# mLSTM cell and leaky-ReLU MLP on one core: p2 first in every group, another order of the sums of x, ScalarE's transfers from unit 8 on, mixed weights behind the masks

## The chip, the cores and the metric

The kernel runs on one core of one Trainium2 chip. Its engines are TensorE (PE, with its weight loads shown apart as PEld), VectorE (DVE), ScalarE (ACT), GpSimd (POOL) and SyncE (SP), which here only issues transfers. The metric is the time of one execution on the device in microseconds (us).

## What is computed

An mLSTM cell runs over 768 tokens of 4 batches and 8 heads (head size 40); its output, 3072 tokens of 320 values, goes through a two-layer MLP:

```
for t in range(S):                       # the cell, per batch and head
    m_new = max(f[t] + m, i[t])
    C = exp(f[t] + m - m_new) * C + exp(i[t] - m_new) * outer(v[t], k[t])
    n = exp(f[t] + m - m_new) * n + exp(i[t] - m_new) * k[t]
    y[t] = sigmoid(o[t]) * (C @ q[t]) / max(abs(n . q[t]), 1)
x = y as (4 * 768, 8 * 40)
h = x @ w_in                             # 320 -> 2048
out = maximum(0.01 * h, h) @ w_out       # 2048 -> 320
```

All values are 32-bit floats.

## The kernel before

The 768 tokens are cut into six chunks of 128. A step s = 4c + b is chunk c of batch b; a group g is the MLP on chunk g of all four batches, 512 tokens. One loop at the end of the kernel interleaves the two: pass c (1 to 6) runs the *units* of group c - 1 in the order of `ffs`, and between them the cell work of chunk c. Pass 1 has 32 units (group 0, ordinary products); passes 2 to 6 have 28 each (groups 1 to 5). `manual_schedule` keeps PE, DVE, ACT and POOL in the order in which the program issues their instructions, so each of these engines is a queue: an instruction that waits holds up all behind it. ACT's queue holds its DMA issues too.

**The MLP of groups 1 to 5** is a Strassen-Winograd product with seven block products, each in two halves n = 0, 1. The first layer's, p1 to p7, are units 0 to 13 (`fast_firsts`); the second layer's, also called p1 to p7, are units 14 to 27 (`fast_units`, in the order p1, p2, p4, p6, p7, p5, p3). In the first layer several products share a chain of PSUM banks, and later products accumulate on what the earlier ones left: p1, p6, p7 and p4 on "u", p2 on "s", p5 and p3 on "v". So the result of p1(n) must have been taken out of its banks (`keep`: two copies on ACT; or `add`: two additions on DVE, and then a leaky ReLU, `relu`, on ACT) before p6(n) may be written on them. One flag, `swapped`, sets the order: in group 1 it is p2, p1, p6, p7, p4, p5, p3, with p2 kept and p1 added; in groups 2 to 5 it is p1, p6, p7, p4, p2, p5, p3, with p1 kept and p2 added. The first layer's matmuls are L946, `add` is L975, `keep` L979, `relu` L971; the second layer's matmuls are L830.

**The sums of x** (`sums_of_x`, L928, POOL) make x3 = b22 - b12, b12 - b11 in place, x2 and x4 out of the blocks of x, three instructions each, issued after the last unit of the group before. p6 reads x2, p7 x3, p4 x4.

**The sums of weights** (`sums_of_weights`, DVE, L908 to L918) are 14 instructions made once, three after each unit of pass 1 from unit 24 on; the last two are L918. **The mixed weights** (`mixed_weights`, POOL, L203 to L206: t3, a12 in place, t2, t4) are four instructions made once in pass 2, one after each of units 10 to 13; the second layer's p4 reads t4, p6 t2 and p7 t3.

**The cell work** of a pass is nine calls: u_parts of two steps after unit 1 (matmuls L629 and L634, then on DVE L639, L639 and L610 for each), u_mix of the two after unit 4 (matmuls L710, then on DVE the chain from L717 to L728, with L606 and L724 on POOL and the tanh L497 on ACT), u_parts of the other two after unit 13, the transposed gates (L332, L337) and u_mix of these after unit 17. From chunk 2 on, `prep_kq` (DVE: L516, L516, L524, L524) prepares a step's operands in pieces of one instruction, so many after each unit; `prep_exp` (L461, ACT) makes a step's exponentials three a unit, after a number of units set in `late`; `prep_mask` (L453, POOL) adds a mask to a step's w before unit 0 (second pair of the chunk) and before unit 12 (first pair of the next chunk), once w has landed. The gates of the next chunk (L283 to L303, DVE) are issued after unit 3 in pass 2 and after unit 0 in later passes.

**The second layer's DVE steps** are L848 and L853 (after p1; block sums of the activations), L857 (after p2), L879 (after p4; p7 reads its result) and L865 (after p6).

**Transfers from ACT's queue** (`feed_slowly`, in `chores`) load w, k and v for the steps four ahead: 14 for each pair of steps, queued when the pair's u_mix is done (units 4 and 17), w first; one is issued after each unit, in pass 2 only from unit 7 on.

Of the kernel before, what the change touches and what calls it, by code (L numbers as in the profile page):

```python
# [13 lines left out]
ALU = mybir.AluOpType  # L14
# [4 lines left out]
def kernel(  # L19
# [26 lines left out]
    nc = tc.nc  # L46
    B, H, S, D = q.shape
    P = 128
# [144 lines left out]
    at = 3 * KH * NH  # L193
    s4_at = raw_l[:, at : at + 8 * P].rearrange("p (n k e t) -> p n k e t", n=2, k=2, e=2)
    dw = raw_l[:, at + 8 * P : at + 12 * P].rearrange("p (n e t) -> p n e t", n=2, e=2)
    x4_at = raw_l[:, at + 12 * P : at + 12 * P + 2 * HT].rearrange("p (k t) -> p k t", t=HT)
    p1_at = [raw_l[:, at + 12 * P + 2 * HT + n * NH :][:, :NH] for n in range(2)]

    def mixed_weights():
# [720 lines left out]
    def sums_of_x(g):  # L920

        xT = st["xT", g]
        for what in range(4):
            for rows, k, a, b in alike:
                b11, b12, b21, b22 = (xT[rows, j, ts(i, HT)] for j in (a, b) for i in range(2))
                x2, x3, x4 = (t[rows, k] for t in (x2_at, x3_at, x4_at))
                to, left, right = ((x3, b22, b12), (b12, b12, b11), (x2, b22, b12), (x4, b21, x2))[what]
                nc.gpsimd.tensor_tensor(to, left, right, op=ALU.subtract)  # L928

    def fast_firsts(g):  # L930

        xT = st["xT", g]
        kept = {}

        def product(n, terms, of):
            if of not in kept:
                kept[of] = [psf.tile([P, 2, HT], F32, name=f"ph{r}", tag="mm")[:] for r in range(2)]
                first = True
            else:
                first = False  # L940
            bank = kept[of]
            for e in range(2):
                for m, (left, right) in enumerate(terms):
                    for r in range(2):
                        rows = ts(r, DP)
                        nc.tensor.matmul(  # L946
                            bank[r][:, e, :], lhsT=left(r)[rows, e], rhs=right(r)[rows],
                            start=first and e == 0 and m == 0, stop=e == 1 and m == len(terms) - 1, skip_group_check=True,
                        )
            return bank  # L950

        def w_at(i, n, at):
            return [lambda r, k=k: w5[:, 2 * i + n, at[r][k]] for k in range(2)]

        def s_at(t, n):
            return [lambda r, k=k: t[:, n, k] for k in range(2)]

        def x_at(at, h):
            return [lambda r, k=k: xT[:, at[r][k], ts(h, HT)] for k in range(2)]

        def t_of(t):
            return [lambda r, k=k: t[:, k] for k in range(2)]

        def rest(i, n, h):
            return [(lambda r: w5[:, 2 * i + n, KX[r]] if i < 2 else dw[:, n], lambda r: xT[:, KX[r], ts(h, HT)])]

        def at(n, i, h):
            return acts[:, KH * i + 4 * n : KH * i + 4 * n + 4, ts(h, HT)]

        def relu(to, z):  # L970
            nc.scalar.activation(to, z, AF.Prelu, alpha=0.01)  # L971

        def add(to, bank):
            for r in range(2):
                nc.vector.tensor_tensor(to[:, 2 * r : 2 * r + 2], to[:, 2 * r : 2 * r + 2], bank[r], op=ALU.add)  # L975

        def keep(to, bank):
            for r in range(2):
                nc.scalar.copy(to[:, 2 * r : 2 * r + 2], bank[r])  # L979

        swapped = g == 1

        def p1(n):
            z = at(n, 0, 0)
            bank = product(n, list(zip(w_at(0, n, K1), x_at(K1, 0))), ("u", n))
            if swapped:
                add(z, bank)
                relu(z, z)
            else:
                keep(z, bank)  # L990

        def p6(n):
            keep(at(n, 0, 1), product(n, list(zip(s_at(s2_at, n), t_of(x2_at))), ("u", n)))

        def p7(n):
            keep(at(n, 1, 1), product(n, list(zip(s_at(s3_at, n), t_of(x3_at))), ("u", n)))

        def p4(n):
            bank = product(n, list(zip(w_at(1, n, K2), t_of(x4_at))) + rest(1, n, 0), ("u", n))
            for r in range(2):  # L1000
                relu(at(n, 1, 0)[:, 2 * r : 2 * r + 2], bank[r])

        def p2(n):
            z = at(n, 0, 0)
            bank = product(n, list(zip(w_at(0, n, K2), x_at(K2, 0))) + rest(0, n, 0), ("s", n))
            if swapped:
                keep(z, bank)
            else:
                add(z, bank)
                relu(z, z)  # L1010

        def p5(n):
            z = at(n, 1, 1)
            add(z, product(n, list(zip(w_at(1, n, K1), x_at(K1, 1))) + rest(1, n, 1), ("v", n)))
            relu(z, z)

        def p3(n):
            z = at(n, 0, 1)
            add(z, product(n, list(zip(s_at(s4_at, n), x_at(K2, 1))) + rest(2, n, 1), ("v", n)))
            relu(z, z)  # L1020

        order = (p2, p1, p6, p7, p4, p5, p3) if swapped else (p1, p6, p7, p4, p2, p5, p3)
        return [lambda p=p, n=n: p(n) for p in order for n in range(2)]

    def u_gates(c):
        gates_T(c, bus.pop(c)[0])
# [20 lines left out]
    def ahead(s):  # L1047

        if s < NS:
            if s < 2 * B:  # L1050
                u_split(s)
            if s >= 2 * B:
                late[s] = 5 if 2 * B + 2 <= s < 3 * B else 3
            lazy[s] = prep_exp(s)
            if s < 2 * B:
                prep_qs(s)
                load_next(s)
            else:
                fine[s] = prep_kq(s)
            state_next(s, 0)  # L1060
            prep_vu(s)
            if s + 1 <= 2 * B:
                prep_mask(s + 1)
# [104 lines left out]
    with tc.manual_schedule(engines={E.PE, E.DVE, E.Activation, E.Pool}):  # L1168
# [23 lines left out]
        for c in range(1, NB + 1):  # L1192
# [6 lines left out]
            for i in range(n_ff):  # L1199
# [14 lines left out]
                    if c * B + n < NS:  # L1214
                        prep_mask(c * B + n)
                ffs[i]()
                for _ in range(1 if c > 2 and i < N1 else 2 if i > 5 else 0):
                    while fine and next(fine[min(fine)], fine) is fine:
                        del fine[min(fine)]
                if c == 1 and i >= 24:  # L1220
                    run(sums, 3)
                if c == 2 and i == 10:
                    mixes = mixed_weights()
                if c == 2 and i >= 10:
                    next(mixes, None)
                if i == n_ff - 1 and c < NB:
                    sums_of_x(c)
                if chores and (c != 2 or i > 6):
                    while chores and next(chores[0], chores) is chores:
                        chores.pop(0)  # L1230
                if c + 1 < NB:
                    if i == (1, 3, 0)[min(c, 3) - 1]:
                        gates(c + 1)
                    if i == (3, 4, 2)[min(c, 3) - 1]:
                        gates_exp(c + 1)
                upto = min(n_c, sum(p <= i for p in (place if c == 1 else pairs)))
# [65 lines left out]
```

## Time and profile before

| | before |
|---|---|
| runs | 495.93, 500.71 and 500.74 us; median 500.71 |
| profiled execution | 496.93 us, span 495.1 us, mean granted PE clock 0.972 |
| PE busy | 480.3 us (97%) |
| DVE busy | 353.7 us (71%) |
| ACT busy | 203.7 us (41%) |
| POOL busy | 199.8 us (40%) |
| group 1, first layer | 138.8 to 183.3 us of the span |
| group 2, first layer | 216.85 to 254.6 us |
| group 5, first layer | 430.1 to 461.45 us |

The span is the time from the first to the last instruction of the profiled execution; the execution's own time is 1.83 us longer. Rows of the trace give the start of a group of instructions in us from the span's start, their busy time, engine, line, operation, what is written from what, shapes and number; in square brackets stand the idle time of the engine before them and what ended it. A name such as L946 is line 946 of the kernel before.

### The profile page before, as it was taken

Reading aid. Unit: us, or ns where it says so; the run is one execution under the profiler, and the core shown is the slowest. Engines: PE = TensorE matmul, PEld = TensorE weight load, DVE = VectorE, ACT = ScalarE, POOL = GpSimd, SP = SyncE. Lnnn points to the kernel's source line nnn. Section 1 sums busy time; section 2 is a strip of 40 time slices with the busy share of each in tenths; the row PEclk is TensorE's granted clock in tenths of the full one; section 3 lists DMA queues with packets and bytes.
Section 4 is the critical chain, followed back from the end, with each engine's and each line's share of the span. In section 5 each row is a group of like instructions: output and inputs, shape, how many; then the busy total and the mean of one; then the engine's idle time right before and its main releaser. Section 6 shows DMA issues by size and latency. Waiting matters only on the chain.

```text
span 495.1 us, 14022 instructions
## 1 busy us (share of the span) xinstructions
PE 480.3 (97%) x5621; PEld 433.5 (88%) x5621; DVE 353.7 (71%) x585; ACT 203.7 (41%) x508; POOL 199.8 (40%) x239
## 2 busy tenths in 40 slices
PE   8997999999998899999999999999999999999997
PEld 7896788867787789998899998899989899988997
DVE  4759998898999967786787886787737787104641
ACT  3465865742635351155631335620344611153210
POOL 4142743452385961494412694203583003700020
PEclk9568999999999989999999999999999999999999
DMA  9977786898761573486584685663865211200001
GB/s 115 161 193 160 168 209 163 173 187 169 158 142 26 135 149 80 115 167 151 145 152 96 150 170 118 174 124 93 156 161 128 54 56 46 87 1 1 2 1 54
DMA packets 165297, 59.31 MB, mean 120 GB/s; under 512 B 128816, under 2 KB 156016, under 8 KB 165232
## 3 DMA queue, kind: packets, MB, share of 16 engines
q1 hardware_dynamic: 125104, 51.20, 46.0%
q10 hardware_dynamic: 40128, 7.21, 9.2%
q8 instruction: 44, 0.72, 0.6%
q14 instruction: 21, 0.17, 0.1%
HBM read 51.68 MB, written 6.70 MB: 118 GB/s over the span
## 4 chain that ended last, share of the span: by engine, by line
PE 70%; DVE 11%; SPq 9%; DMA 4%; ACT 3%; issue 2%; POOL 0%; ACTq 0%; DVEq 0%; POOLq 0%
PE po L830 31%; PE ph L946 27%; SPq L233 4%; PE pT L710 3%; PE sd L629 2%; PE po L796 2%; SPq L358 2%; PE ph L774 2%; DVE qn L524 1%; SPq L372 1%; DVE qn L639 1%; ACT kqT L554 1%; PE sd L634 1%; DMA w<-a_dr 1%; DMA rb<-in_q_dram 1%
## 5 line engine op out<-in xcount | busy, mean ns | idle before, releaser
L830 PE MATMUL po<-w_out,acts 128*128 128x160 f32 x640 | 89.1, 300 | 0.0
L830 PEld LDWEIGHTS po<-w_out,acts 128*128 128x128 f32 x640 | 87.3, 190 | 0.6 <-ACT acts L971 0.3
L946 PE MATMUL ph<-xT,w_in 64*128 64x256 f32 x720 | 82.7, 378 | 0.0
L946 PEld LDWEIGHTS ph<-xT,w_in 64*128 64x128 f32 x720 | 69.2, 187 | 8.9 <-issue 0.7
L975 DVE TENSOR_TENSOR acts<-acts,ph 128x512 f32<-128x512 f32 x60 | 38.3, 682 | 41.6 <-PE ph L946 41.5
L830 PE MATMUL po<-raw,acts 128*128 128x160 f32 x480 | 66.4, 300 | 0.0
L830 PEld LDWEIGHTS po<-raw,acts 128*128 128x128 f32 x480 | 65.4, 190 | 0.3
L606 POOL TENSOR_TENSOR S<-S,f 40x336 f32<-40x336 f32 x36 | 31.6, 879 | 75.7 <-PE pT L710 35.9
L461 ACT ACTIVATE w<-w,gT 128x64 f32<-128x64 f32 (+1 forms) x192 | 51.7, 346 | 15.7 <-DMA w<-a_dr 4.6
L979 ACT COPY acts<-ph 128x512 f32<-128x512 f32 x60 | 32.1, 587 | 46.7 <-PE ph L946 46.7
L971 ACT ACTIVATE acts<-acts 128x1024 f32<-128x1024 f32 x30 | 31.7, 1056 | 43.6 <-DVE acts L975 43.4
L774 PE MATMUL ph<-xT,w_in 64*128 64x256 f32 x320 | 38.6, 392 | 1.2 <-ACT acts L782 1.2
L946 PE MATMUL ph<-acts,w 64*128 64x256 f32 x320 | 37.5, 382 | 1.8 <-DVE acts L975 1.8
L453 POOL TENSOR_TENSOR w<-w,i 128x512 f32<-128x512 f32 x20 | 27.7, 1394 | 26.2 <-DMA w<-a_dr 14.3
L774 PEld LDWEIGHTS ph<-xT,w_in 64*128 64x128 f32 x320 | 31.6, 193 | 5.7 <-ACT acts L782 1.6
L796 PE MATMUL po<-w_out,acts 128*128 128x320 f32 x128 | 36.5, 437 | 0.0
L946 PEld LDWEIGHTS ph<-acts,w 64*128 64x128 f32 x320 | 31.2, 187 | 5.7 <-POOL w L453 2.2
L724 POOL TENSOR_TENSOR xb<-xb,den 128x320 f32<-128x320 f32 x16 | 11.6, 727 | 60.5 <-DVE xb L721 58.1
L639 DVE TENSOR_TENSOR qn<-w,sd 64x512 f32<-64x512 f32 x40 | 27.3, 684 | 8.2 <-PE sd L629 4.5
L796 PEld LDWEIGHTS po<-w_out,acts 128*128 128x128 f32 x128 | 23.6, 190 | 9.3 <-issue 0.3
L863 POOL TENSOR_TENSOR y<-y,raw 128x160 f32<-128x160 f32 x10 | 9.5, 950 | 54.5 <-DVE acts L865 44.0
L946 PE MATMUL ph<-xT,raw 64*128 64x256 f32 x240 | 29.0, 394 | 1.7 <-DVE acts L975 1.7
(169 smaller groups left out, 810.8 us busy)
## 6 DMA issues: line engine op xcount, KB each, us to landing
rb<-in_k_dram SPq DMA_DIRECT2D x64, 80.0 KB
rb<-in_q_dram SPq DMA_DIRECT2D x64, 80.0 KB
rb<-in_o_gate_dram SPq DMA_DIRECT2D x64, 80.0 KB
ea<-a_dr SPq DMA_DIRECT2D x32, 128.0 KB
raw<-in_moe_w_out_dram SPq DMA_DIRECT2D x6, 640.0 KB
w<-a_dr ACTq DMA_DIRECT2D x24, 128.0 KB
xT<-x_dr SPq DMA_DIRECT2D x32, 96.0 KB
acts<-in_moe_w_in_dram SPq DMA_DIRECT2D x20, 128.0 KB
```

The lines of the kernel that those rows point to most:

```text
L233: nc.sync.dma_start(to[DP * r : DP * (r + 1), 2 * P * slot : 2 * P * (slot + 1)], src[r, :, SLOTS[r][slot], :],)
L453: nc.gpsimd.tensor_tensor(w, w, cm2.unsqueeze(1).to_broadcast([P, H, SL]), op=ALU.add)
L461: yield nc.scalar.activation(w[:, h, :], w[:, h, :], AF.Exp, bias=gT[c][:, 0, bh : bh + 1], scale=1.0)
L606: nc.gpsimd.tensor_tensor(new, old, g, op=ALU.mult)
L639: nc.vector.tensor_tensor(mixed(s)[toks, u], w[toks], bank[1 - u][toks], op=ALU.mult)
L774: nc.tensor.matmul(ph[r][:, cols], lhsT=w_row(r, slot, j), rhs=xT[DP * r : DP * (r + 1), slot, cols], start=(slot == 0), stop=(slot == KC ...
L796: nc.tensor.matmul(po[n][:], lhsT=acts[:, f, ts(n, P)], rhs=w_out[:, f, :], start=(f == 0), stop=(f == NF - 1),)
L830: nc.tensor.matmul(bank[:], lhsT=left[:, f, :], rhs=right[:, f, :], start=f == 0, stop=f == KH - 1)
L946: nc.tensor.matmul(bank[r][:, e, :], lhsT=left(r)[rows, e], rhs=right(r)[rows], start=first and e == 0 and m == 0, stop=e == 1 and m == le ...
L971: nc.scalar.activation(to, z, AF.Prelu, alpha=0.01)
L975: nc.vector.tensor_tensor(to[:, 2 * r : 2 * r + 2], to[:, 2 * r : 2 * r + 2], bank[r], op=ALU.add)
L979: nc.scalar.copy(to[:, 2 * r : 2 * r + 2], bank[r])
```

## The change

`swapped` is gone: every group from 1 on has the order p2, p1, p6, p7, p4, p5, p3, keeps p2 (ACT) and adds p1 (DVE). The sums of x become x1 = b12 - b11 (in the place where x4 was), x2 = b22 - x1 and x3 = b22 - b12, nine instructions at the end of the group before; the fourth, b21 - x2, is made in place by `last_sum_of_x` right after p2(1), which reads b21 unchanged. p4 now reads b21's place, p5 reads x1.

In the loop, the pieces of `prep_kq` come one a unit before unit 14 and two after, in every pass (before: in pass 2 none to unit 5, then two). Of the weight sums of pass 1 the last two (L918) are issued in pass 2 after unit 3, behind the gates. The four mixed weights are issued together after unit 12 of pass 2, behind both masks of that unit. ACT's transfers are issued from unit 8 on: one a unit to unit 13, then two. In `late`, steps 14, 15, 18, 19, 22 and 23 get 5 units in place of 3.

The instructions of each engine stay the same in kind and number, apart from the order and the operands named here; the order of SP's queue does not change.

```diff
--- before.py
+++ after.py
@@ -193,7 +193,7 @@
     at = 3 * KH * NH
     s4_at = raw_l[:, at : at + 8 * P].rearrange("p (n k e t) -> p n k e t", n=2, k=2, e=2)
     dw = raw_l[:, at + 8 * P : at + 12 * P].rearrange("p (n e t) -> p n e t", n=2, e=2)
-    x4_at = raw_l[:, at + 12 * P : at + 12 * P + 2 * HT].rearrange("p (k t) -> p k t", t=HT)
+    x1_at = raw_l[:, at + 12 * P : at + 12 * P + 2 * HT].rearrange("p (k t) -> p k t", t=HT)
     p1_at = [raw_l[:, at + 12 * P + 2 * HT + n * NH :][:, :NH] for n in range(2)]
 
     def mixed_weights():
@@ -920,12 +920,18 @@
     def sums_of_x(g):
 
         xT = st["xT", g]
-        for what in range(4):
+        for what in range(3):
             for rows, k, a, b in alike:
-                b11, b12, b21, b22 = (xT[rows, j, ts(i, HT)] for j in (a, b) for i in range(2))
-                x2, x3, x4 = (t[rows, k] for t in (x2_at, x3_at, x4_at))
-                to, left, right = ((x3, b22, b12), (b12, b12, b11), (x2, b22, b12), (x4, b21, x2))[what]
+                b11, b12, b22 = xT[rows, a, :HT], xT[rows, a, HT:], xT[rows, b, HT:]
+                x1, x2, x3 = (t[rows, k] for t in (x1_at, x2_at, x3_at))
+                to, left, right = ((x1, b12, b11), (x2, b22, x1), (x3, b22, b12))[what]
                 nc.gpsimd.tensor_tensor(to, left, right, op=ALU.subtract)
+
+    def last_sum_of_x(g):
+
+        for rows, k, a, b in alike:
+            b21 = st["xT", g][rows, b, :HT]
+            nc.gpsimd.tensor_tensor(b21, b21, x2_at[rows, k], op=ALU.subtract)
 
     def fast_firsts(g):
 
@@ -978,16 +984,10 @@
             for r in range(2):
                 nc.scalar.copy(to[:, 2 * r : 2 * r + 2], bank[r])
 
-        swapped = g == 1
-
         def p1(n):
             z = at(n, 0, 0)
-            bank = product(n, list(zip(w_at(0, n, K1), x_at(K1, 0))), ("u", n))
-            if swapped:
-                add(z, bank)
-                relu(z, z)
-            else:
-                keep(z, bank)
+            add(z, product(n, list(zip(w_at(0, n, K1), x_at(K1, 0))), ("u", n)))
+            relu(z, z)
 
         def p6(n):
             keep(at(n, 0, 1), product(n, list(zip(s_at(s2_at, n), t_of(x2_at))), ("u", n)))
@@ -996,22 +996,18 @@
             keep(at(n, 1, 1), product(n, list(zip(s_at(s3_at, n), t_of(x3_at))), ("u", n)))
 
         def p4(n):
-            bank = product(n, list(zip(w_at(1, n, K2), t_of(x4_at))) + rest(1, n, 0), ("u", n))
+            bank = product(n, list(zip(w_at(1, n, K2), x_at(K2, 0))) + rest(1, n, 0), ("u", n))
             for r in range(2):
                 relu(at(n, 1, 0)[:, 2 * r : 2 * r + 2], bank[r])
 
         def p2(n):
-            z = at(n, 0, 0)
-            bank = product(n, list(zip(w_at(0, n, K2), x_at(K2, 0))) + rest(0, n, 0), ("s", n))
-            if swapped:
-                keep(z, bank)
-            else:
-                add(z, bank)
-                relu(z, z)
+            keep(at(n, 0, 0), product(n, list(zip(w_at(0, n, K2), x_at(K2, 0))) + rest(0, n, 0), ("s", n)))
+            if n == 1:
+                last_sum_of_x(g)
 
         def p5(n):
             z = at(n, 1, 1)
-            add(z, product(n, list(zip(w_at(1, n, K1), x_at(K1, 1))) + rest(1, n, 1), ("v", n)))
+            add(z, product(n, list(zip(w_at(1, n, K1), t_of(x1_at))) + rest(1, n, 1), ("v", n)))
             relu(z, z)
 
         def p3(n):
@@ -1019,8 +1015,7 @@
             add(z, product(n, list(zip(s_at(s4_at, n), x_at(K2, 1))) + rest(2, n, 1), ("v", n)))
             relu(z, z)
 
-        order = (p2, p1, p6, p7, p4, p5, p3) if swapped else (p1, p6, p7, p4, p2, p5, p3)
-        return [lambda p=p, n=n: p(n) for p in order for n in range(2)]
+        return [lambda p=p, n=n: p(n) for p in (p2, p1, p6, p7, p4, p5, p3) for n in range(2)]
 
     def u_gates(c):
         gates_T(c, bus.pop(c)[0])
@@ -1050,7 +1045,7 @@
             if s < 2 * B:
                 u_split(s)
             if s >= 2 * B:
-                late[s] = 5 if 2 * B + 2 <= s < 3 * B else 3
+                late[s] = 5 if s % B > 1 else 3
             lazy[s] = prep_exp(s)
             if s < 2 * B:
                 prep_qs(s)
@@ -1214,23 +1209,23 @@
                     if c * B + n < NS:
                         prep_mask(c * B + n)
                 ffs[i]()
-                for _ in range(1 if c > 2 and i < N1 else 2 if i > 5 else 0):
+                for _ in range(1 if i < N1 else 2):
                     while fine and next(fine[min(fine)], fine) is fine:
                         del fine[min(fine)]
-                if c == 1 and i >= 24:
+                if c == 1 and 24 <= i < 28:
                     run(sums, 3)
-                if c == 2 and i == 10:
-                    mixes = mixed_weights()
-                if c == 2 and i >= 10:
-                    next(mixes, None)
+                if c == 2 and i == 12:
+                    run(mixed_weights())
                 if i == n_ff - 1 and c < NB:
                     sums_of_x(c)
-                if chores and (c != 2 or i > 6):
+                for _ in range(0 if i < 8 else 1 if i < N1 else 2):
                     while chores and next(chores[0], chores) is chores:
                         chores.pop(0)
                 if c + 1 < NB:
                     if i == (1, 3, 0)[min(c, 3) - 1]:
                         gates(c + 1)
+                        if c == 2:
+                            run(sums)
                     if i == (3, 4, 2)[min(c, 3) - 1]:
                         gates_exp(c + 1)
                 upto = min(n_c, sum(p <= i for p in (place if c == 1 else pairs)))
```

## The prediction

> **What bounds the kernel now.** I read the page's first lines, then busy time by stretches, then the waits of TensorE (PE), then the rows of VectorE (DVE) and GpSimd (POOL) around those waits. The page says who is nearly always busy:
>
> ```profile
> span 495.1 us, 14022 instructions
> PE 480.3 (97%) x5621; PEld 433.5 (88%) x5621; DVE 353.7 (71%) x585; ACT 203.7 (41%) x508; POOL 199.8 (40%) x239
> ```
>
> So only PE's idle or slowed time can be won. Busy time by stretches (length, then busy time of PE, PEld, DVE, ACT, POOL, then the granted clock) shows where that is; the rows are the first-layer part of groups 1, 2, 3, 4 and 5:
>
> ```profile
> 138.80:183.30 44.50, 40.99 (x609) 35.01 (x609) 38.06 (x56) 20.90 (x47) 32.86 (x27) 0.96 0.50 117
> ...
> 216.85:254.60 37.75, 37.75 (x609) 33.50 (x608) 27.93 (x49) 20.50 (x48) 17.45 (x21) 1.00 0.68 149
> ...
> 288.15:325.90 37.75, 37.75 (x610) 33.50 (x609) 27.92 (x49) 19.85 (x44) 17.45 (x21) 1.00 0.67 155
> 359.40:397.30 37.90, 37.90 (x546) 34.08 (x545) 22.96 (x41) 19.05 (x40) 15.20 (x20) 1.00 0.48 113
> 430.10:461.45 31.35, 31.35 (x290) 27.87 (x289) 6.75 (x11) 13.90 (x21) 2.96 (x5) 1.00 0.02 7
> ```
>
> Groups 2 to 5 are solid PE at full clock. Group 1, the one that already starts with p2, is 44.50 - 37.75 = 6.75 us longer for the same products. PE's rows there:
>
> ```profile
> 151.75 2.50 PE L946 MATMUL ph<-acts,w 64*128 64x256 f32 x16 [1.81 <-DVE acts L975]
> ...
> 173.72 7.64 PE L946 MATMUL ph<-xT,raw 64*128 64x256 f32 x48 [1.71 <-DVE acts L975]
> ```
>
> The first is p6(0), waiting for the adds of p1(0) on DVE; the second is p3, waiting for the adds of p5(0), and it then runs slowly (7.64 us; 48 such matmuls take 5.2 elsewhere: 31.35/290 each). Why DVE is late, DVE first, then POOL:
>
> ```profile
> 147.29 1.38 DVE L639 TENSOR_TENSOR qn<-w,sd 64x512 f32<-64x512 f32 x2
> ...
> 150.94 2.47 DVE L975 TENSOR_TENSOR acts<-acts,ph 128x512 f32<-128x512 f32 x4
> ...
> 167.69 5.26 DVE L524 TENSOR_TENSOR qn<-kqT,ea 64x512 f32<-64x512 f32 x2
> 172.97 2.48 DVE L975 TENSOR_TENSOR acts<-acts,ph 128x512 f32<-128x512 f32 x4
> ```
>
> ```profile
> 165.73 3.35 POOL L203 TENSOR_TENSOR raw<-w_out 128x1280 f32<-128x1280 f32 x1
> 169.16 3.23 POOL L204 TENSOR_TENSOR w_out<-w_out 128x1280 f32<-128x1280 f32 x1
> 172.35 1.72 POOL L453 TENSOR_TENSOR w<-w,i 128x512 f32<-128x512 f32 x1
> 178.16 1.27 POOL L453 TENSOR_TENSOR w<-w,i 128x512 f32<-128x512 f32 x1 [4.09 <-DMA rb<-in_k_dram]
> 179.39 2.92 POOL L205 TENSOR_TENSOR raw<-w_out 128x1280 f32<-128x1280 f32 x1
> 182.38 2.92 POOL L206 TENSOR_TENSOR raw<-w_out,raw 128x1280 f32<-128x1280 f32 x1
> ```
>
> Two L524, 0.72 each by their median, took 5.26 us while POOL mixed weights (L203, L204), and the pair ends 0.56 after L204 does: each waited out a whole POOL instruction. The last two mixes, L205 and L206, met only DVE work that reads PSUM (L975, L639), and nothing was slowed.
>
> **Part 1: group 1's late adds.** Two L918 (2.25 us) leave DVE's queue before group 1 and return behind gates(3). L639 then starts when its matmuls allow: 1.35 after u_parts' start at 144.17 (group 2: 221.82 - 220.47), at 145.5 and not 147.29. Lower down, L203 and L204 no longer lie beside L524, and DVE's cell steps go one a unit, so p5's adds come in time as in groups 2 to 4. If all of that goes: -6.75. Bounds: -4.0 (p3's wait and slow matmuls alone: 1.88 + 2.1) and -6.75.
>
> **Part 2: p2, p1, p6 in groups 2 to 5.** PE's matmuls are the same. Before, p1's banks were emptied by ScalarE copies (0.59 each), with u_parts between p1 and p6. After, u_parts sits between p2 and p1, and p6(0) waits for DVE's adds of p1(0), queued behind L639 x2, L610, L639 x2, L610. With u_parts starting at U: L639 at U+1.35, queue empty at U+5.05 (group 2: 225.5 - 220.47), adds until U+6.3. PE is ready for p6 at U + 2.1 (u_parts) + 3.5 (p1) = U+5.6. In group 1, p6(0) ended 1.9 after its second add (152.2 to 154.1), so now at U+8.2 against U+7.35 undisturbed: 0.9 late. The same holds in group 1. Groups 1 to 4: +3.6. Group 5 has no u_parts: the adds (1.3) fit under p1(1) (1.7), but ScalarE now has two relus of 1.06 ahead of p6(0)'s copy, and p7(0) needs that: +0.3. Bounds a group: 0 (adds in time) and 2.6 (what group 1 paid: p6(0) at 154.1, not 151.5).
>
> **Part 3: sums of x.** Nine POOL subtractions at the group's end, not twelve, then three after p2(1). x2, the first that PE needs, is sixth, not ninth, and p6 comes later: hidden, cost 0. The three late ones (0.85 each) wait for p2(1); queued behind them is u_mix's state step, which waits for PE until some 5 us later. p7(1) and p4 need them over 10 us later. If that cover went, p4 would wait by what is missing.
>
> **Part 4: ScalarE's transfers.** None before unit 8, one to unit 13, then two. The same 28 issues a group at 0.4 to 0.7 us. They leave units 0 to 7, where ScalarE empties PE's banks; before, no copy there made PE wait in groups 2 to 5, so nothing is won. Six value transfers now stand in a row ahead of the tanh (L497): three took 2.25 us (at 259.27), six take 4.5, the tanh ends near 264.7, and L721 wants it at 266.8. Cost 0; bounds 0 and a rival below. `late` moves the exponentials of steps 14, 15, 18, 19, 22 and 23 two units on, still ahead of u_parts: 0. SyncE's queue keeps its order, instruction for instruction.
>
> **Part 5: the mixes behind the masks.** The second mask of unit 12 needs the fourth w transfer, issued at relu p5(1). Call the PE end of p5(1) E. In this program that is about 170.0: 144.2 + u_parts 2.1 + p1 3.5 + p6(0) 2.6 + u_mix 2.1 + 72 slots of 0.216 (p6(1), p7, p4, p5). Then adds to E+1.9, transfer 3.8 (174.30 to the mask at 178.16), mask 1.27: the mixes start near E+7.1. Alone they last 11.7 (4 x 2.92). DVE reaches L848 at U' + 5.1 = E+10.3 (U' is u_parts at E+5.2). L848 x2 and L853 x2 read SBUF twice, like L524, so I take them to alternate with the mixes: two L848 (1.13) slip between, the mixes end at E+7.1+11.7+2.3, less 0.4 for hand-overs (L524, once free, took 0.56 and not 0.72): E+20.7. PE wants t4 for p4(0) at E + 5.2 (p3) + 2.1 + 8.95 (p1, p2) + 2.65 = E+18.9: wait **1.8**. The two L853, L606 of POOL between them and the four small DVE steps end near E+24.4; before, that point was free at 193.3, with PE's p4(0) at 194.9. From u_mix's first transpose (L717, 194.07) to the end of the first L879 (201.75 + 1.21) are 8.9 us of DVE work: L879 ends at E+33.3. p7(0) needs it and stands 8.8 after p4(0), at E+29.5: wait **3.8**. Bounds of the two together: 0 (mixes done early) and 7.5 (the w transfer held 2.1 us, as ScalarE was between 165.35 and 167.98).
>
> What an idle PE does to its clock, by stretches of 3.4 us before and after the gaps:
>
> ```profile
> 150.30:153.70 3.40, 1.95 (x15) 1.59 (x16) 3.37 (x8) 1.32 (x2) 2.41 (x2) 1.00 0.00 0
> 170.80:174.20 3.40, 1.69 (x14) 1.03 (x10) 3.37 (x4) 0.00 (x0) 3.27 (x2) 1.00 0.71 157
> 174.20:177.60 3.40, 3.40 (x17) 2.68 (x18) 1.25 (x3) 3.31 (x8) 0.00 (x0) 0.50 0.64 174
> ```
>
> A stretch with PE busy for 1.69 was followed by half clock, one with 1.95 was not. A wait of 3.8 leaves at most 1.5 in one of the two stretches it falls in, so I add half a stretch at half clock, 3.4 / 2 = 1.7, rounded to **1.8** for hand-over. The 0.9 of part 2 trips nothing. Bounds: 0, and 3.5 (both waits trip).
>
> The Trainium skill, "TensorE: Matmul & The Clock Gate", section "What's actually happening", gives the cold state to at least one idle window of about 3.4 us. The trace differs: 1.7 us idle sufficed. By the page the sum below would be 1.8 lower, 499.7. On part 5 the skill's "SBUF — State Buffer", section "Who interferes with whom", says that a two-SBUF-input DVE instruction and a SBUF-reading GpSimd one exclude each other for the whole instruction. The trace agrees (L524: 5.26 for two); taken as a mere slowdown of 5.26/1.44 = 3.7 for the time of the mixes, the four would still end with the mixes, so the sum stays.
>
> **The sum**, against the profiled execution's own 496.93 (span 495.1 and 1.83 around it): 496.93 - 6.75 + 3.6 + 0.3 + 1.8 + 3.8 + 1.8 = **501.5**. The runs shown are 495.93, 500.71 and 500.74; the profiled one lies 3.8 below their median, and the trace can't say which step makes that difference, so I add nothing for it. Measured against the median, 500.71, the forecast is no change; 1% (about what a measurement of this kernel can tell from none) reaches from 495.7 to 505.7.
>
> **Rivals.**
> - *The mixes cost nothing* (fourth transfer early, or DVE not excluded): 496.93 - 6.75 + 3.9 = 494.1. For it: L205 and L206 cost nothing before. Against it: they ended at 185.3, a microsecond before L848; now they start where they ended. 17%.
> - *p1's adds come in time*: 501.5 - 3.6 = 497.9, if ScalarE and DVE clear their queues 0.9 earlier. Against it: L639 and L610 run back to back. 8%.
> - *Slower: p6(0) waits 2.6 in groups 2 to 4*, as in group 1 before, and half of these waits trip the clock: 501.5 + 3 x 1.7 + 2 x 1.8 = 510.2. It takes 1.7 us more DVE work ahead of L639; the gate steps (3.9 us beside POOL's sums, done at 221.1) have 2.4 to spare. 10%.
> - *Slower: the six value transfers hold the tanh*. L497 may end 0.7 after L721's time, L879's slack in group 2; that is 1.2 us a transfer. With three held 2.1 each, 2.9 a group, in four groups: 513. One was held so before, at 165.35. 8%.
> - *The change doesn't do what it says*: p3's wait stays in group 1, 501.5 + 4.0 = 505.5. 5%.
>
> **Numbers.** The sum itself gets 52%: 10 above 505.7 (both waits trip the clock, transfer held), 42 within 1%. Faster by over 1%: 17. Within: 42 + 8 + 5 = 55. Slower: 10 + 10 + 8 = 28. The range 493.5 to 507 leaves out the two slow rivals (18). The likeliest case's own range is 498 to 507.
>
> **What would show it.** Group 1's first-layer stretch near 38.6 us, without p3's wait; a wait of PE for L981 (the adds' new line) of under a microsecond at p6(0) in groups 1 to 4; L203 to L206 in a row after both masks, with L848 and L853 stretched beside them; PE idle at p4(0) and, longer, at p7(0) of group 1, half clock behind. If L848 starts before the mixes or after they end, part 5 is wrong; if p6(0) never waits, part 2 is.

## The result and the profile after

| | runs | median us | from - to |
|---|---|---|---|
| before | 6 | 499.05 | 495.93 - 503.92 |
| after | 6 | 505.01 | 504.07 - 508.41 |

The kernel after takes 1.0142 of the time before (95% interval 1.0093 to 1.0192): 1.4% slower. Every ratio here and below leaves out runs more than 1.5% above the fastest of their kernel (here before's 503.92) and is taken against runs of before made beside them, so it is not the quotient of two medians of these tables. The profiled execution of after took 508.41 us (span 506.6), the longest of its six runs; it lies 11.5 above the profiled execution of before, where the medians are 6.0 apart. In the page's first lines PE has the same work in a longer span:

```profile
span 506.6 us, 14039 instructions
...
PE 480.8 (95%) x5621; PEld 434.6 (86%) x5621; DVE 362.1 (71%) x585; ACT 202.5 (40%) x508; POOL 201.2 (40%) x239
```

Busy time by stretches of after (length, then PE, PEld, DVE, ACT, POOL, granted clock, DMA share and GB/s): group 1's first and second layer, then the first layers of groups 2 to 5.

```profile
143.19:182.12 38.93, 38.92 (x609) 34.71 (x608) 33.08 (x55) 19.68 (x46) 20.75 (x23) 1.00 0.41 105
182.12:225.88 43.76, 36.03 (x298) 35.42 (x294) 36.89 (x44) 8.17 (x28) 30.13 (x24) 0.88 0.66 124
225.88:264.41 38.53, 38.50 (x609) 33.67 (x608) 27.87 (x49) 19.76 (x44) 17.01 (x20) 1.00 0.54 129
297.93:336.46 38.53, 38.49 (x609) 33.66 (x608) 28.77 (x48) 19.64 (x44) 17.42 (x21) 1.00 0.56 137
369.98:408.44 38.46, 38.46 (x545) 33.66 (x544) 23.29 (x40) 18.91 (x40) 13.96 (x18) 1.00 0.43 103
441.28:472.86 31.58, 31.58 (x289) 30.00 (x288) 6.94 (x12) 13.79 (x21) 2.26 (x4) 1.00 0.02 7
```

The second line's counterpart before:

```profile
183.30:216.82 33.52, 33.52 (x299) 33.07 (x295) 27.40 (x44) 6.58 (x25) 16.51 (x19) 1.00 0.53 117
```

Group 1's first layer is 5.6 us shorter, the first layers of groups 2 to 5 are together 2.4 longer, and group 1's *second* layer, in which the diff moves nothing on PE, is 10.2 longer, with less than full clock. PE's rows there show one wait:

```profile
191.70 1.15 PE L710 MATMUL pT<-qn,S 128*64 128x64 f32 x32
200.58 1.98 PE L710 MATMUL pT<-qn,S 128*64 128x64 f32 x32 [7.73 <-DVE f L344]
```

The second step's transposes need the PSUM bank that held tg, and DVE's copies of tg (L342, L344) free it. They are late because of what stands ahead of them in DVE's queue. DVE, then POOL:

```profile
184.72 0.50 DVE L610 TENSOR_TENSOR S<-S,sd 40x336 f32<-40x336 f32 x1
185.14 6.92 DVE L848 TENSOR_TENSOR acts<-acts 128x1024 f32<-128x1024 f32 x2
191.98 7.72 DVE L853 TENSOR_TENSOR acts<-acts 128x1024 f32<-128x1024 f32 x2
199.63 0.54 DVE L857 TENSOR_TENSOR y<-raw,po 128x160 f32<-128x160 f32 x2
200.09 0.21 DVE L342 COPY gT<-tg 128x64 f32<-128x64 f32 x1
200.23 0.21 DVE L344 COPY f<-tg 128x64 f32<-128x64 f32 x1
```

```profile
178.24 1.27 POOL L453 TENSOR_TENSOR w<-w,i 128x512 f32<-128x512 f32 x1 [8.28 <-DMA w<-a_dr]
183.01 1.27 POOL L453 TENSOR_TENSOR w<-w,i 128x512 f32<-128x512 f32 x1 [3.50 <-DMA w<-a_dr]
184.24 2.89 POOL L203 TENSOR_TENSOR raw<-w_out 128x1280 f32<-128x1280 f32 x1
187.21 3.76 POOL L204 TENSOR_TENSOR w_out<-w_out 128x1280 f32<-128x1280 f32 x1
191.06 3.75 POOL L205 TENSOR_TENSOR raw<-w_out 128x1280 f32<-128x1280 f32 x1
194.89 3.74 POOL L206 TENSOR_TENSOR raw<-w_out,raw 128x1280 f32<-128x1280 f32 x1
```

The pairs L848 and L853 took 2.34 and 2.35 us before; now 6.92 and 7.72. The mixes begin at 184.24, 0.9 ahead of the first L848, and each mix and each addition (one L848 or L853) waits for the other's end in turn: L203 ends at 187.13, the first L848 can only then run its 1.1, L204's 3.76 hold that 0.8, and so on for four rounds. The granted clock by stretches of 3.4 us:

```profile
191.90:195.30 3.40, 0.95 (x32) 0.81 (x28) 3.40 (x2) 0.83 (x2) 3.32 (x2) 1.00 0.89 152
195.30:198.70 3.40, 0.00 (x0) 0.00 (x0) 3.40 (x2) 0.00 (x0) 3.33 (x1) 0.50 0.11 31
198.70:202.10 3.40, 1.52 (x29) 1.55 (x30) 3.30 (x10) 0.00 (x0) 1.63 (x1) 0.50 0.00 0
202.10:205.50 3.40, 3.40 (x20) 3.28 (x18) 2.87 (x7) 0.00 (x0) 1.49 (x2) 0.50 0.24 64
```

So the 10.2 us are about 7.9 of wait (7.73 and the hand-over) and 2.3 of half clock once PE works again.

Group 1 itself starts 4.4 us later in this pair of profiles (143.19 for 138.78). PE waits in pass 1 for L267 on DVE (the row is below); the next section asks whether the change makes that.

```profile
133.11 1.83 PE L796 MATMUL po<-w_out,acts 128*128 128x320 f32 x4 [3.02 <-DVE w_out L267]
```

### The profile page after: what moved, and what is told of

It reads as the page before. It is cut to its first block, busy times and chain, and to the rows that moved or that the text cites. A ratio compares the mean times of both kernels' runs of the same rounds, so it can differ in the third digit from the quotient of the medians.

```text
span 506.6 us, 14039 instructions
## 1 busy us (share of the span) xinstructions
PE 480.8 (95%) x5621; PEld 434.6 (86%) x5621; DVE 362.1 (71%) x585; ACT 202.5 (40%) x508; POOL 201.2 (40%) x239
## 4 chain that ended last, share of the span: by engine, by line
PE 76%; DVE 8%; SPq 7%; DMA 3%; issue 3%; ACT 1%; POOL 1%; ACTq 0%; DVEq 0%; POOLq 0%
PE ph L952 32%; PE po L830 29%; PE po L796 4%; PE pT L710 3%; PE sd L629 3%; PE ph L774 2%; SPq L233 2%; SPq L358 2%; DMA rb<-in_q_dram 1%; SPq L363 1%; SPq L372 1%; PE sd L634 1%; DVE raw L265 1%; DMA rb<-in_o_gate_dram 1%; DVE acts L853 1%
## 5 line engine op out<-in xcount | busy, mean ns | idle before, releaser
L830 PE MATMUL po<-w_out,acts 128*128 128x160 f32 x640 | 89.1, 300 | 0.0
L830 PEld LDWEIGHTS po<-w_out,acts 128*128 128x128 f32 x640 | 87.3, 190 | 0.6 <-issue 0.3
L952 PE MATMUL ph<-xT,w_in 64*128 64x256 f32 x720 | 86.6, 379 | 0.0
L952 PEld LDWEIGHTS ph<-xT,w_in 64*128 64x128 f32 x720 | 71.4, 187 | 8.2 <-issue 0.5
L830 PE MATMUL po<-raw,acts 128*128 128x160 f32 x480 | 67.9, 304 | 0.0
L830 PEld LDWEIGHTS po<-raw,acts 128*128 128x128 f32 x480 | 66.8, 193 | 0.3
L981 DVE TENSOR_TENSOR acts<-acts,ph 128x512 f32<-128x512 f32 x60 | 38.1, 680 | 40.2 <-PE ph L952 39.9
L453 POOL TENSOR_TENSOR w<-w,i 128x512 f32<-128x512 f32 x20 | 26.6, 1341 | 43.7 <-DMA w<-a_dr 43.3
L796 PE MATMUL po<-w_out,acts 128*128 128x320 f32 x128 | 38.1, 450 | 3.0 <-DVE w_out L267 3.0
L952 PE MATMUL ph<-acts,w 64*128 64x256 f32 x320 | 39.2, 382 | 0.1
L774 PE MATMUL ph<-xT,w_in 64*128 64x256 f32 x320 | 38.1, 390 | 0.2 <-DVE w_in L267 0.2
L639 DVE TENSOR_TENSOR qn<-w,sd 64x512 f32<-64x512 f32 x40 | 27.4, 684 | 14.8 <-PE sd L634 7.6
L952 PEld LDWEIGHTS ph<-acts,w 64*128 64x128 f32 x320 | 32.0, 187 | 5.6 <-issue 1.2
L774 PEld LDWEIGHTS ph<-xT,w_in 64*128 64x128 f32 x320 | 31.4, 192 | 4.5 <-DVE w_in L267 0.3
L524 DVE TENSOR_TENSOR qn<-kqT,ea 64x512 f32<-64x512 f32 x32 | 26.9, 841 | 0.8
```

The lines of the kernel that those rows point to most:

```text
L453: nc.gpsimd.tensor_tensor(w, w, cm2.unsqueeze(1).to_broadcast([P, H, SL]), op=ALU.add)
L524: nc.vector.tensor_tensor(mixed(s)[rows, 1 - r], d["kqT"][rows, 1].rearrange("p (h t) -> p h t", t=SL), d["ea"][rows], op=ALU.mult,)
L639: nc.vector.tensor_tensor(mixed(s)[toks, u], w[toks], bank[1 - u][toks], op=ALU.mult)
L774: nc.tensor.matmul(ph[r][:, cols], lhsT=w_row(r, slot, j), rhs=xT[DP * r : DP * (r + 1), slot, cols], start=(slot == 0), stop=(slot == KC ...
L796: nc.tensor.matmul(po[n][:], lhsT=acts[:, f, ts(n, P)], rhs=w_out[:, f, :], start=(f == 0), stop=(f == NF - 1),)
L830: nc.tensor.matmul(bank[:], lhsT=left[:, f, :], rhs=right[:, f, :], start=f == 0, stop=f == KH - 1)
```

## Experiments

Theory 1: the loss is made in group 1's second layer by the mixes beside L848 and L853, as read above. Rival 1: it is the late transfers of w from ScalarE's queue, behind which masks and mixes stand. Rival 2: it is the new order of the products, through waits at p6(0). The table has every profile's stages: start of group 1, its two layers, the first layers of groups 2 to 5 together, all in us (the other second layers are 33.52, 33.52, 32.84 and 30.69 in all of them, to 0.02). "Lead" is from the first mix to the first L848, "wait" PE's wait for L344.

| kernel | start | first | second | 2 to 5 | lead | wait | median, ratio to before (95%) |
|---|---|---|---|---|---|---|---|
| before | 138.78 | 44.52 | 33.52 | 144.69 | - | 0 | |
| before, again | 140.94 | 47.96 | 33.52 | 144.96 | - | 0 | |
| after | 143.19 | 38.93 | 43.76 | 147.10 | 0.90 | 7.73 | 505.01, 1.0142 (1.0093 - 1.0192) |
| after, again | 140.07 | 39.88 | 43.31 | 147.16 | 0.88 | 7.75 | |
| mixes ahead of masks | 144.54 | 39.56 | 33.52 | 147.10 | 16.33 | 0 | 497.23, 0.9952 (0.9914 - 0.9990) |
| mixes in halves | 141.19 | 40.08 | 39.37 | 147.09 | 1.31 | 1.77 | 502.92, 1.0075 (1.0040 - 1.0109) |
| mixes one a unit | 139.20 | 39.66 | 34.93 | 147.09 | 15.96 | 1.19 | 496.58, 0.9982 (0.9945 - 1.0018) |
| old order of products | 142.53 | 40.09 | 42.72 | 144.45 | 1.37 | 7.17 | 502.09, 1.0058 (1.0020 - 1.0095) |
| mixes alone moved, in before | 141.01 | 42.86 | 39.83 | 144.75 | 6.70 | 3.11 | 499.24, 0.9995 (0.9947 - 1.0042) |
| the same, again | 140.20 | 44.37 | 35.35 | 144.93 | 5.84 | 0 | |
| old transfers | 141.16 | 41.42 | 35.35 | 147.09 | 5.97 | 0 | 501.22, 1.0040 (1.0000 - 1.0080) |
| the same, again | 138.31 | 41.15 | 40.44 | 147.09 | 5.44 | 4.11 | |
| mixes ahead, old order | 141.78 | 40.91 | 33.52 | 144.46 | 16.34 | 0 | 495.34, 0.9924 (0.9886 - 0.9962) |
| the same, p1 first in group 1 | 139.69 | 42.50 | 33.52 | 144.48 | 19.21 | 0 | 496.87, 0.9953 (0.9920 - 0.9987) |

**Mixes ahead of the masks.**

```diff
+                if c == 2 and i == 12:
+                    run(mixed_weights())
                 for n in masks.get(i, ()) if 1 < c < NB else ():
...
-                if c == 2 and i == 12:
-                    run(mixed_weights())
```

> The kernel after, with one edit: the four mixed weights are issued at unit 12 ahead of its two masks instead of behind them. Theory 1 (the mixes run beside DVE's two-SBUF-input adds L848 and L853, each waiting for whole GpSimd instructions; L342 and L344 then free the transposes' bank late, PE waits 7.7 us for it in group 1's second layer and runs 10 us at half clock): GpSimd starts the mixes some 10 us earlier and is through before L848; group 1's second layer falls from 43.8 to 33.5-35 us; at most 1-2 us come back as a wait for p5's adds behind L524. Total 8 to 10 us below the kernel after, so 495-497, ratio to before 0.99 to 1.0. Rival 1 (the late transfers of w from ScalarE's queue are the cause, the mixes only stand behind them): the masks and what follows are as late as before, the second layer stays above 40 us, total 503-505. Rival 2 (the new order of the products is the loss, through waits at p6): total within 2 us of the kernel after, 503-506.

POOL and DVE of this run:

```profile
171.08 3.36 POOL L203 TENSOR_TENSOR raw<-w_out 128x1280 f32<-128x1280 f32 x1
174.51 2.91 POOL L204 TENSOR_TENSOR w_out<-w_out 128x1280 f32<-128x1280 f32 x1
177.50 3.23 POOL L205 TENSOR_TENSOR raw<-w_out 128x1280 f32<-128x1280 f32 x1
180.81 3.25 POOL L206 TENSOR_TENSOR raw<-w_out,raw 128x1280 f32<-128x1280 f32 x1
184.02 2.50 POOL L453 TENSOR_TENSOR w<-w,i 128x512 f32<-128x512 f32 x2
```

```profile
174.69 3.28 DVE L524 TENSOR_TENSOR qn<-kqT,ea 64x512 f32<-64x512 f32 x1
179.19 2.09 DVE L524 TENSOR_TENSOR qn<-kqT,ea 64x512 f32<-64x512 f32 x1
187.41 2.35 DVE L848 TENSOR_TENSOR acts<-acts 128x1024 f32<-128x1024 f32 x2
189.68 2.35 DVE L853 TENSOR_TENSOR acts<-acts 128x1024 f32<-128x1024 f32 x2
```

The mixes are through 3.3 us before L848; the four additions take their own time, and the second layer is 33.52, though the masks now begin only at 184.02 (178.24 in after). Two single L524, one a unit, are stretched to 3.28 and 2.09, and no addition of p5 is late for PE. Rival 1 in its plain form (late masks cost PE time) and rival 2 (only 2 us to be had) fall: one call moved ahead takes the ratio from 1.0142 to 0.9952.

**Mixes in halves.** Each mix is two instructions of 128x640, behind the masks as in after.

> The kernel after, with each of the four mixes cut into two instructions of half the columns, in the same place behind the masks. Theory 1 with the exclusion for whole instructions: each L848 and L853 waits out half a mix only, some 1.5 to 1.9 us, in place of 3.1 to 3.9; the chain of four ends 4 to 7 us earlier, PE's wait for the transposes' bank falls from 7.7 to between 1 and 4 us, the half clock behind it is shorter or gone; group 1's second layer 34.5 to 39 us, total 498-501. If DVE is only slowed in proportion to GpSimd's busy time (no exclusion by instruction), the split changes nothing: 43-44 us and 504-506. Rival 1 (late transfers): unchanged too.

```profile
193.75 1.98 PE L709 MATMUL pT<-qn,S 128*64 128x64 f32 x32 [1.77 <-DVE f L343]
197.32 3.01 PE L829 MATMUL po<-raw,acts 128*128 128x160 f32 x10 [1.59 <-POOL raw L205]
```

(Lines are numbered one lower in this kernel: L343 is L344, L709 is L710, L829 is L830; all mixes are L205.) The same work in smaller instructions cuts the wait from 7.73 to 1.77: the exclusion is by the instruction. But POOL's mixes now end 57.6 us after the group's start (55.4 in after), and p4, which PE reaches earlier, waits 1.59 for t4 (the wait that the prediction had placed there); with the two waits the granted clock falls to 0.50 (193.8 to 197.2), and the layer is 39.37, just above the range expected; the total missed it by 2 us.

**Mixes one a unit, as before.** `next(mixes)` after each of units 10 to 13.

> The kernel after, with the mixes issued one after each of units 10 to 13 as in the kernel before. Theory 1: the first two run beside L524 (two SBUF inputs as well; p5's adds late, PE's wait of 1 to 2 us at p3 returns), the last two stand behind the masks and now meet the first L848s: second layer of group 1 between 36 and 41 us, first layer 39 to 42 us; total 499-503, between the kernel after and the one with the mixes ahead of the masks. Rival 1 (late transfers alone): second layer above 42 us, total 503-506. Rival: the place of the mixes is all and the old one was free of cost: second layer 33.5, total 495-496.

Better than expected, and by its interval not to be told from before: the first two run beside L524, and still p3 does not wait. The rows suggest why, the operands' pieces come one a unit and the L524 stand apart, but no run changes that alone. Of the last two mixes, the end of one and the whole of the next meet the two L848 (the third mix begins 2.0 before them), and PE waits 1.19 for L344, with no loss of clock.

**The old order of the products** (`swapped` and the sums of x as in before, all else as in after).

> The kernel after, with the order of the products and the sums of x as in the kernel before (groups 2 to 5 begin with p1, which ScalarE copies; group 1 with p2); mixes behind the masks, transfers, the late L918 and the pace of the pieces stay as in the kernel after. Theory 1: the first layers of groups 2, 3 and 4 go back from 38.5 to 37.75 us and that of group 5 from 31.6 to 31.3; the second layer of group 1 stays near 43.8; total 2 to 3 us below the kernel after, 502-503.5. Rival 2 (the order is the main loss): total 496-499.

As theory 1 has it: groups 2 to 5 give back 2.65 us (147.10 to 144.45), the second layer of group 1 stays at 42.72 with its 7.17 of wait. The order costs about what was forecast (3.0), a quarter of what group 1's second layer loses.

**The mixes alone, in the kernel before:** together at unit 12, behind the masks.

> The kernel before, with one edit: its four mixed weights are issued together at unit 12 behind the two masks instead of one after each of units 10 to 13. Theory 1: L524 is free of the mixes, so p3's wait for p5's adds and its slow matmuls go from group 1's first layer (44.5 to 40-41.5 us); but the mixes now run from about 179 to 191 and beyond, across L848 and L853, so PE waits 4 to 8 us for the transposes' bank and the second layer goes from 33.5 to 40-44 us. Sum: 2 to 6 us above the kernel before, 501-505. Rival 1 (late transfers are the cause; here they are not gated until unit 7 and come early): mixes done in time, second layer 33.5, total 4 us below the kernel before.

Half right. p3's wait is gone and the second layer is 39.83 here, but p6(0) still waits 2.7 (42.86), and the total, expected 2 to 6 us higher, is that of before, with runs from 495.1 to 506.8. The profiled execution, 503.89, is one of the longest, so its stages need not be those of the median.

**The old transfers, in the kernel after** (`if chores and (c != 2 or i > 6):` in place of the loop from unit 8).

> The kernel after, with ScalarE's transfers paced as in the kernel before (one a unit; in pass 2 only from unit 7 on); all else as in the kernel after. Theory 1: the masks may come up to 3 us earlier and the mixes with them, but they still lie across L848 and L853; group 1's second layer falls by no more than 3-4 us, 40-44 us, total 502-505. Rival 1 (the gated transfers are the cause): mixes done before L848, second layer 33.5-35, total 495-497.

Theory 1 missed here: 35.35, not 40 to 44. The second mask starts 37.2 us after the group (39.8 in after), the mixes 6.0 before L848 and not 0.9. POOL, then DVE:

```profile
182.62 2.91 POOL L204 TENSOR_TENSOR w_out<-w_out 128x1280 f32<-128x1280 f32 x1
185.62 7.36 POOL L205 TENSOR_TENSOR raw<-w_out 128x1280 f32<-128x1280 f32 x1
193.05 2.90 POOL L206 TENSOR_TENSOR raw<-w_out,raw 128x1280 f32<-128x1280 f32 x1
```

```profile
185.60 2.35 DVE L848 TENSOR_TENSOR acts<-acts 128x1024 f32<-128x1024 f32 x2
187.87 2.35 DVE L853 TENSOR_TENSOR acts<-acts 128x1024 f32<-128x1024 f32 x2
```

Here L848 began 0.02 us ahead of L205, and DVE kept POOL out over all four additions (L205 took 7.36). PE only waited 1.76 for t4 from L206. The kernel's runs spread from 496.7 to 505.3, so this kernel and the previous one were each profiled again:

> The kernel after with ScalarE's transfers as before, unchanged, profiled once more, since its runs spread from 496.7 to 505.3 us. In the first profile the first L848 began 0.02 us ahead of the third mix, and DVE then ran all four adds in a row (1.2 us each) while that mix took 7.4 us: PE paid 1.8 us. Theory (who begins first keeps the other out): if a mix is under way again when L848 is issued, the adds and the mixes alternate, 3 to 4 us an add, and the second layer of group 1 takes 38 to 43 us; if an add is first, 35 to 36 us. Rival (with the mixes 4 us earlier the collision is always cheap): 35 to 36 us whatever the order, and the spread is that of the start of group 1.

> The kernel before with the mixes alone behind the masks, unchanged, profiled once more, since its runs spread from 495.1 to 506.8 us. First profile: mixes from 180.2, L848 issued at 186.9 while the third ran, adds and mixes alternated for two adds, second layer of group 1 39.8 us. Theory: the second layer is set by the number of mixes still to come when L848 is issued: four 43 to 44, two 39 to 40, none 33.5 us; if an add begins between two mixes, 35 to 36. Rival: 39.8 us again, whatever the places.

The old transfers again, where L848 (182.47) met L204 under way since 180.04: POOL, DVE, PE.

```profile
180.04 2.91 POOL L204 TENSOR_TENSOR w_out<-w_out 128x1280 f32<-128x1280 f32 x1
183.03 3.76 POOL L205 TENSOR_TENSOR raw<-w_out 128x1280 f32<-128x1280 f32 x1
186.87 3.76 POOL L206 TENSOR_TENSOR raw<-w_out,raw 128x1280 f32<-128x1280 f32 x1
```

```profile
182.47 5.40 DVE L848 TENSOR_TENSOR acts<-acts 128x1024 f32<-128x1024 f32 x2
187.80 5.62 DVE L853 TENSOR_TENSOR acts<-acts 128x1024 f32<-128x1024 f32 x2
```

```profile
194.30 1.98 PE L710 MATMUL pT<-qn,S 128*64 128x64 f32 x32 [4.11 <-DVE f L344]
```

The same kernel, 40.44 in place of 35.35. And the mixes alone, again, went the other way: L848 at 187.58, L205 at 187.73 and 7.24 long, second layer 35.35. So with a lead near 6 us, a few tenths decide between a wait of 1.8 and one of 3 or 4; with the lead of 0.9 that after has in both its profiles, all four additions alternate with mixes. Rival 1 thus holds a part: the gated transfers cost nothing by themselves (group 1's first layer is even shorter with them, see part 4 below), but they set the lead.

**Before and after, once more.**

> The kernel before, unchanged, profiled once more. If the spread of its runs (494.8 to 505.4 us) is made in pass 1, where the weights' transfers land, group 1 starts anywhere between 138.5 and 145 us of the span, and the stretches behind it repeat: 44.5, 33.5, 37.8, 33.5, 37.7, 33.5, 37.9, 32.8, 31.3, 30.7 us, each to 0.3. If the spread is made in group 1 itself, its first layer differs by over 1 us.

> The kernel after, unchanged, profiled once more. Theory 1: first layer of group 1 39 to 40 us, second 42 to 44 us with a wait of 6 to 8 us for the transposes' bank behind four stretched L848 and L853; groups 2 to 4 at 38.5. The start of group 1 lies anywhere between 138.5 and 145 us if the difference of 4.4 us found there between the two kernels is chance, near 143 if the change makes it.

Both places vary. The start of group 1 lies between 138.31 and 144.54 over the 14 profiles, 138.78 to 140.94 for the one kernel before, 140.07 to 143.19 for the one kernel after: two profiles of each cannot tell the 4.4 us of the first pair from chance. The wait for L267 in pass 1, 3.02 in after's first profile, stands in before's second profile too, with 2.2, so the change is not needed for it. And before's group 1 was 3.4 us longer in its second profile, with the same two waits, 5.3 us together and not 3.5, and half clock behind (the row gives total, number and longest):

```profile
PE ph L946 <- DVE acts L975: 5.3, 2, 3.5
```

**The two gains together** (mixes ahead of the masks, old order), and the same with p1 first in group 1 too:

> The kernel after, with two edits together: mixes ahead of the masks, and the order of products and sums of x of the kernel before. Theory 1, by the stages of the two runs that made one edit each: group 1 first layer 39.5-40, second 33.5; groups 2 to 4 37.7, group 5 31.3; 2.4 us below the kernel with the mixes ahead of the masks alone: 494-495.5, ratio to before 0.987-0.992. If the two gains overlap, 497.

> The same two edits, with p1 first in group 1 as well (p1 copied by ScalarE, p2 added by DVE, in all groups). Theory 1: p6(0) then waits for no adds of DVE in any group, and group 1's first layer comes to 37.8-38.5 us, 1 to 2 us below the run with p2 first in group 1: 492.5-494.5. Rival: the weights' last sums or w_in's blocks are not ready for p1 so early or ScalarE's copies stand behind other work at the start of group 1, and PE waits there instead: 496 or more.

The first is the best kernel found, 0.9924 (0.9886 to 0.9962) of before: 495.34, within what was expected, though its first layer, 40.91, is 0.9 longer than the 40 expected at most. The second took the time of its rival, but not for the rival's reasons (weight sums, w_in's blocks, ScalarE's copies): p6(0) comes so early that it waits for POOL's sums of x (L928), and half clock follows (first layer 42.50).

```profile
PE ph L946 <- POOL acts L928: 1.3, 1, 1.3
```

## Why the prediction was right or wrong

The forecast was 501.5, 4.6 us above the profiled time of before; measured was 505.01, 6.0 above the median. That lies within the stated range, 493.5 to 507, but two steps of the sum failed (parts 4 and 5), so the total is right in part by luck. By stages, with the means of the two profiles of each kernel: -6.8 (group 1's first layer), +10.0 (its second), +2.3 (groups 2 to 5) make +5.5; forecast were -5.85, +7.4 and +3.0. The 2.6 that the second layer cost beyond its forecast were partly paid back by the two others. The mean of -6.8 stands for a -5.6 in the first pair of profiles and a -8.1 in the second.

- **Part 1, -6.75: right.** The stretch was to be 38.6 with the 0.9 at the group's own p6(0); it is 38.93 and 39.88, without p3's wait. The size depends on which execution of before is taken: 44.52 or 47.96. For p3 it suffices to move the mixes (the kernel before with the mixes alone moved has no wait there). The pieces one a unit seem to suffice too (after with the mixes one a unit has no wait either), but that run differs from before in more than the pieces. The bound of 4.0 for p3 alone is 4.1 by the row shown: 1.71 of wait, not 1.88, and 7.64 less 5.2.
- **Part 2, +3.6 and +0.3: right.** +0.74, +0.80 and +0.57 in groups 2 to 4 and +0.30 in group 5, gone when the old order is put back. PE's rows of groups 2 to 5 list no wait, for its matmuls overlap; the delay shows in p6(0) itself (L981 and L952 are L975 and L946 of before; DVE, then PE, group 2):

```profile
236.22 2.47 DVE L981 TENSOR_TENSOR acts<-acts,ph 128x512 f32<-128x512 f32 x4
```

```profile
237.04 2.50 PE L952 MATMUL ph<-acts,w 64*128 64x256 f32 x16
```

The two additions of p1(0) end at 236.90 and 237.49, and p6(0) starts on the first of its banks at 237.04 and on the second at 237.55; its 16 matmuls take 2.50, where 32 take 3.73. In group 1 the wait was below 1 in the first profile and 1.3 in the second, where the weight sums that stay in pass 1 (L911) ran until 148.0, right up to L639, so that there L639 did not start "when its matmuls allow".
- **Part 3, 0: right.** No run with the new order shows a wait of PE's matmuls for the sums of x; in three of them one weight load waits 0.3 us for the last sum.
- **Part 4, 0: wrong.** The step that failed is the zero itself: the prediction has "nothing is won", and nothing lost, when the transfers leave units 0 to 7. ScalarE's queue issued the first w 27.2 us after the group's start (23.4 before), and the second mask came 2.3 to 3.5 us later than with the old transfers (39.8 and 40.8 against 37.2 and 37.5 after the group's start). Alone that costs nothing, as the run with the mixes ahead of the masks shows; with the mixes behind the masks it took their lead over L848 from some 5.7 to 0.9 us. The prediction's mixes started at E+7.1; they started at E+9.8 (E, the end of p5(1), is near 174.4). Most of that is the fourth w transfer, forecast at E+1.9 and issued at 179.45, E+5.05: ScalarE had stood on the issue of the second w from 172.09 to 174.41, and the exponentials then ran ahead of p5(1)'s relu. Something was won, too: in both profiles with the old transfers PE waits in p5 for a relu on ScalarE, 0.85 and 0.89, and group 1's first layer takes 41.42 and 41.15; in the five profiles with the same order and gated transfers that wait is not there and it takes 38.93 to 40.08.
- **Part 5, +7.4: mechanism right, place wrong.** Mixes and additions alternated as forecast. The step that failed is the list of who waits: "PE wants t4 for p4(0)" and then L879 for p7(0). DVE's queue holds something that PE wants earlier than either, the copies L342 and L344, since the second step's transposes reuse tg's bank. Ahead of them stand all four additions, so the whole delay fell on one wait of 7.73; p4 and p7 then found everything ready. The prediction followed data and forgot a bank: it did count the copies (among "the four small DVE steps" that end near E+24.4) but did not ask who waits for them. By its own figures PE would have wanted the bank a good 1 us before p4(0), near E+17.9, so its waits would have come to about 6.5 there (an estimate) instead of 1.8 and 3.8.
- **Clock, 1.8: right in size**; what the second layer lost beyond the wait is 2.3. The run with the 1.19 wait shows no half clock. The prediction's reading, that the busy time of a stretch tells, does not hold up (last section).
- **Rivals.** In the second layers of groups 2 to 5, 33.52, 33.52, 32.84 and 30.69 before and after, no wait for the tanh appears, so the six value transfers held nothing up. (The price of that rival does not follow from its terms: three times 2.1, less 2.8 of slack, is 3.5 a group, not 2.9.) Nor did p6(0) wait 2.6 anywhere in after.
- **The level.** The sum was taken against an execution 3.8 below the median of the runs shown and read as "no change" against that median. What makes before's two profiles differ is mostly the length of group 1's first layer (3.4 us), which the change cuts, and the start of group 1 (2.2), which it leaves. With +5.5 on the median of before, 499.05, the stages give 504.5, half a microsecond from the measured 505.01; with two profiles of each kernel, part of that closeness is chance. Of the 3.5 us between forecast and result, 2.1 are thus the level (499.05 against 496.93) and 0.9 the stages.

The Trainium skill, "SBUF — State Buffer", section "Who interferes with whom", says that the order of issue, not the shape, decides who blocks, and (of VectorE's two-port modes) that whoever issues first gets the shared port pair for the whole instruction. The runs agree on the order: with POOL first, an L848 or L853 took up to 3.9 us; with DVE first, one mix took 7.2 to 7.4. In that second case the mix was kept out over four instructions of DVE and not one, so the measurement goes beyond the sentence.

## What to carry to other kernels

Work moved to another engine's queue has a time of day as well as a cost: note what the other engine runs at that time, and place it by what it collides with, not behind a transfer that may land late. When an engine's queue is delayed, list all that stands behind in it in order, copies that only free a buffer too, and ask for each who wants it first. Where a kernel's own runs spread by 2%, profile it twice before its stages are compared, and add a change to the stage, not to the total of one execution.

## What the runs showed of the hardware that was not expected

- DVE can hold GpSimd out over several instructions: L205 took 7.36 and 7.24 us beside four additions in a row that lost nothing. When an addition found a mix under way, the two engines alternated from then on, one instruction each. Why the turn does not change in the first case is open.
- An operation with one SBUF input seems to be held too: L648 (128x16, 0.17 alone) took 1.87 us in two runs and ended 0.02 to 0.03 after the end of the mix L206 beside it. Here it is after old transfers:

```profile
194.11 1.87 DVE L648 TENSOR_SCALAR den<-hb 128x16 f32<-128x16 f32 x1
```

- After a stretch with 0.95 us of PE work in 3.40 the clock was halved, and a stretch with 1.52, already at half clock, kept it there: three stretches, 195.3 to 205.5, for one wait of 7.73. But the busy time of a stretch cut by hand does not settle what follows: in the kernel with p1 first in group 1, one with 2.06 (144.0 to 147.4) was followed by 0.63, while before had one with 1.95 (150.3 to 153.7) and full clock behind it.
